# A second batch on scaled 16-bit halves in a two-batch attention and two-layer kernel

## The chip, the cores and the metric

The kernel runs on one core of a Trainium2 chip. The metric is the device time of one execution in microseconds, the median over several runs.

## The reference, cut to what matters

```python
def _attn_ref(q, k, v, proj):                   # q, k, v: (2, 8, 768, 64)
    q_bucket = sum((q @ proj > 0) * powers)     # 6 bits of a sign projection
    k_bucket = sum((k @ proj > 0) * powers)
    scores = where(q_bucket == k_bucket, scale * q @ k.T, -1e9)
    attn = softmax(scores)
    return attn @ v

x = attn_out.transpose(0, 2, 1, 3).reshape(1536, 512)
h = x @ w_in                                    # 512 x 2048
g = where(h >= 1, h, where(h <= -1, 0, (h + 1) ** 2 / 4))
x = g @ w_out                                   # 2048 x 512
h = x @ w_in2
out = (h - tanh(h)) @ w_out2
```

So there are two batches of 768 tokens. Each goes through attention with 8 heads and then through two layers, each of which is a wide product (512 to 2048), a pointwise function and a narrow product (2048 to 512). The four weight matrices arrive in 64 bits and each is cut into 16 blocks of 128 x 512.

## The kernel before, in words

**The work.** Tokens lie along the free dimension, so that a 128 x 768 tile is one chunk of features for one batch, and a matrix product has 128 x 128 weights and 384 moving columns (half of the 768 tokens). The precision of 32 bits is kept by splitting: each operand x becomes a high half and a low half, x = hi + lo, and a product takes three matmuls, hi*hi, hi*lo and lo*hi. For the two layers both halves are of the type `float32r` (the profile writes fp32r, or f32 on the operands of TensorE): weights in `WH`/`WL`, inputs of a layer in `XH`/`XL`, the values between its two products in `GH`/`GL`. ScalarE or VectorE makes the high half by a copy, and VectorE or GpSimd the low half by a subtraction (`copy_hi`, `sub_lo`, `w_split`). Only the product of the attention probabilities with v runs on 16-bit halves (`prep_v16`, `pv`, L631), scaled by a power of two that `prep_v` derives from the largest |v| of a pair of heads.

**The stages.** Attention of the first batch comes first (about 0 to 130 us), then the first batch's two layers with the second batch's attention woven in between, then, from 474 us on, the second batch's two layers alone. In the first batch's layers the units are "i" (a chunk of the wide product, `mats` L866, then `post`) and "o" (a part of the narrow product, accumulated in `accs` by L985). In the second batch the wide product is done in units "s": seven products of half-size blocks take the place of eight (`products`, L897), over sums of input chunks (`TF`, split in `thl`) and sums of weight blocks (`w_mix`, L810, split in `cwhl`), and its results are put together by `plus` (L902). There are 8 "s" units and 16 "o" units per layer.

**Weights.** The first use of a block narrows it from 64 bits (`w_narrow`, L786 to L789) into one of four buffers `WR` and stores the narrowed block in device memory (`scr`); later uses load it from there. A block then is split into `whl(n)`. The first batch has three such slots, and the second batch four, of which it shares three with the first.

**The order.** Every operation is recorded once by `op` or `one`, with the engines that may do it and a planner's cost in ns for each. A packed string, `SCHEDULE`, gives the final order of all items and the engine of each; each engine runs its items in that order. The order was found outside of the kernel by a search, with those costs. All DMAs are issued from SP's queue. `SPINS` puts 64 groups of four small 16-bit matmuls (L1127) at places that the order chooses.

Of the kernel before, what the change touches and what calls it, by code (L numbers as in the profile page):

```python
# [35 lines left out]
    "a})!2z@#ALqgkB`mBl>(d6o*M*uQ1lH%r>)Zn!4r3Y`eh@$_}_Z<QO9Uqs{MButNnbPJ~>u==F8o+@3l>5EiMtI0_qp_oAJjld`y8FEaK^lfnyLc*QonrM~~"
    "?}KaIb8Pi$V%s!toSo(Okh|Bg^!Wa9a>ulU(b3U2#mLY0JUl1_#Xso1@gRF}N1Z*e{p0Kgs9pc8I9a_%$fuu1!S`PaNWZoB3%4Kt#y5`B+g{bLyz&`+X73YJ"
    "8Mhqq-;w-~DfEZV@(0go=IYbVQ_MDLtY6rukB3B2$;9v2?5q5U>vH`mW5ub@Xm(Thg;S@#dF*EKd3J<z{v<oZ7^tskc;H2gJg?;=>eMOqFbKhs$%70jdmhP`"
    "#qlRzApDq_Gc$OYBO*CY4O*Re+(i4+cprA*(U*_u8;*j4=Z-)I;8QHMZ5!JP=`HueJ-6IT4wz!@3SeLRBm3ZX=zxO<AJj4fABG>@&-0S+h7=EOylW&PMxQKf"
    "CL~R;L#7dWxts;Did;W+%f_3N6|l?X{7tqU1Be}KW>v1XVe_6<>SoAH*%Gwc&31+D>_%vtis*EHQ+7po4QvR=_$cu@NKAt2Y_(1x*Ipe#kjrHW+I#gnSX=L*"  # L40
    "P^(b_HJ5kcGD<UK2z~<x3WZ*5kIT2!?(3=XS`BL)DxE;fG}qx!VmYa9TFbKZ`lyl~U^68`ix2hm&=MIO8%r1a6^*k4lydG<B7JICpxohbLNq0-dUMk527yK1"
    "HR9v$e7P)wAWJw_>-DK>wmX*@&oEZ0*eG?cq&@P62~SGesVlbD9r37MTQHpfbCMzNz7q*lDw{QQaUsgtk`SwNg0Dpur7~El#2P!4GTk=s4i|tE+aU%36%bJ>"
    "Bd5Z3x4I9cMAb`7gNzN91>luDTNWf*)0P00a27!*=@f($qumfFpRu7sI7rz|gS&dD=`Khr1VtzIr4VSkP^If=re}2zlrue1S5k~pseALiP-u&fLR(kVxnV=5"
    "vJTdF!$c|AIUej7D{kLW8ihj955w@|klhO|)ZiZIhJT%??LPodDeGg)0Dl__L-!69B&^T(5zc4&R`vBrIbECNhc}qd#<k~WT;Rh~4%y85`uk9i)-?`K4J$Q>"
    "<3eLy?Z=@_ID2?-BV9uW2JU1lKY}y#+9_J!OAbtQ6aJBLj$>?e#oo~oN{8s+ZFs9U?Cn`&s80`0+w~px<mg1T8^NhKlfzDFMDJQQtVgWbVQY3^I}FtO1_A1u"
    "px1P{YSFap4n|6)0wtu4lt*(pPBK9IFqfoo?p2R_qwW;eieXgg?2Iag7*(KX3Z&#Y09hN71Xh`<qQFfD6ls~3Aq44&`zosYA+NfcJKRE<S8YmZrBo`LS80@7"
    "q-n%y;4tc1j^i0R$F!D8qs&PZ8dBvn=Mc50ISW}pJ#YrV$TU1g)v1K`GReQ!Q_2YWG+;W;#c`CxkwMuuqZuVC3>8>5IF@6&kM@<9^%P4(-fp871Tpb#&nGSf"
# [80 lines left out]
def lsh_attention_moe_kernel(ctx: ExitStack, tc: tile.TileContext, qT, kT, vR, projR, eye, w1, w2, w3, w4, out, nbits):  # L128
# [39 lines left out]
    vsm = bufs("vsm", B * NP, [128, 8], F32)  # L168
# [29 lines left out]
    WT = PB[0][:, 3 * 128:4 * 128]  # L198
# [11 lines left out]
    GHX, GLX = GH + Ak, GL + Bk  # L210
# [12 lines left out]
    def late(tag, a, b):  # L223

        if tag not in later:
            later[tag] = sb.tile([128, {"w64": 5120}.get(tag, 2 * KC * SH // 2)], FR, name=f"late_{tag}", tag=tag)
        return later[tag][:, a:b]

    def whl(n):

        return (WH[n], WL[n]) if n < 3 else (late("w64", 3840, 4352), late("w64", 4352, 4864))
# [8 lines left out]
    def halves(t):  # L240
        return t.rearrange("p (a b) -> p a b", a=2)

# [52 lines left out]
    def copy_hi(dst, src, ca, cv, reads, writes, cg=None, by=None):  # L295
        if by is not None:
            op([("A", ca + 95.0, lambda: A.activation(dst, src, AF.Copy, scale=by)),
                ("V", cv + 60.0, lambda: V.tensor_scalar(dst, src, by, None, op0=ALU.mult), 1)], reads, writes)
            return
# [154 lines left out]
    def prep_v16(pr):  # L454
        b, hp, _ = pairs[pr]
        f, fc = v_slot(pr)
        n = b * NP + hp
        s, v = vsm[n], v16[0]
        way = vturn[0] % 2
        vturn[0] += 1  # L460
# [461 lines left out]
    def post(u):  # L922
# [76 lines left out]
        elif len(done) == 2 and b:  # L999
# [5 lines left out]
            else:  # L1005
# [9 lines left out]
                for i in range(3):  # L1015
                    split_t(j, i)
# [160 lines left out]
```

## Time and profile before

| what | value |
|---|---|
| runs | 732.95, 730.7, 732.18 us (median 732.18) |
| span of the profiled execution, first to last instruction | 731.3 us |
| TensorE busy | 716.0 us, 98% |
| TensorE weight loads busy | 666.8 us, 91% |
| VectorE, ScalarE, GpSimd busy | 629.3, 480.6, 343.9 us |

No time of the profiled execution itself is listed apart from its span; the span is 0.9 us under the median of the runs. The end of a matmul is modelled in the trace, so successive matmuls overlap in it; how often they start says more than how long each lasts.

### The profile page before, as it was taken

How to read it: one execution, taken by the hardware profiler on the slowest of the kernel's cores; microseconds unless marked ns; L12 is line 12 of the kernel's file. 1: busy time of each engine (PE TensorE's matmuls, PEld its weight loads, DVE VectorE, ACT ScalarE, POOL GpSimd, SP SyncE). 2: the span in 40 equal slices, each digit the busy share in tenths (PEclk: the TensorE clock that was granted, in tenths of full speed). 3: DMA queues.
4: the chain of work that ended last, by engine and by line, in shares of the span. 5: the costliest groups of instructions: out<-in, count | busy, mean ns of one | idle time of the engine just before them, and what ended most of it. 6: DMA issues, size and time to landing. Idle time of an engine off the chain costs nothing.

```text
span 731.3 us, 12554 instructions
## 1 busy us (share of the span) xinstructions
PE 716.0 (98%) x4512; PEld 666.8 (91%) x4512; DVE 629.3 (86%) x1063; ACT 480.6 (66%) x759; POOL 343.9 (47%) x244
## 2 busy tenths in 40 slices
PE   7899999999999999999999999999999999999998
PEld 6577789777999999999999999999999999999997
DVE  7998998988888999999788887988887898988774
ACT  7998898977978778778776777346544535524311
POOL 5874445565545536453445358541324415253430
PEclk9999999999999999999999999999999999999999
DMA  6997988999999798998888967632211311312112
GB/s 192 233 226 274 246 249 274 210 191 229 261 237 266 185 263 219 227 244 231 223 213 233 246 154 161 169 100 90 72 43 60 100 44 57 88 58 73 44 58 87
DMA packets 165102, 124.91 MB, mean 171 GB/s; under 512 B 127232, under 2 KB 135088, under 8 KB 165040
## 3 DMA queue, kind: packets, MB, share of 16 engines
q1 hardware_dynamic: 165040, 124.12, 65.1%
q8 instruction: 35, 0.57, 0.3%
q14 instruction: 27, 0.22, 0.1%
HBM read 73.47 MB, written 19.95 MB: 128 GB/s over the span
## 4 chain that ended last, share of the span: by engine, by line
PE 86%; DVE 5%; DMA 4%; ACT 3%; issue 1%; POOL 1%; SPq 0%; ACTq 0%; DVEq 0%; POOLq 0%
PE mm L866 52%; PE sbk L897 9%; PE pv L897 5%; PE pv L631 4%; PE ss L506 3%; PE ss L510 3%; PE pb L897 2%; DMA pt<-phl 2%; DVE sm L524 2%; PE pb L1127 1%; PE pv L621 1%; PE mm L593 1%; DMA vr<-in_v 1%; DMA pt<-tmp 1%; ACT p L526 1%
## 5 line engine op out<-in xcount | busy, mean ns | idle before, releaser
L798 POOL TENSOR_TENSOR wl<-wr,wh 128x512 fp32r<-128x512 f32 x69 | 96.0, 1398 | 124.8 <-ACT wh L797 62.2
L866 PE MATMUL mm<-gh,wh 128*128 128x384 f32 x396 | 107.2, 338 | 0.0
L866 PE MATMUL mm<-gh,wl 128*128 128x384 f32 x396 | 105.9, 335 | 0.0
L866 PE MATMUL mm<-gl,wh 128*128 128x384 f32 x396 | 105.8, 335 | 0.0
L526 ACT ACTIVATE p<-ss,sm 128x768 f32<-128x768 f32 x78 | 77.2, 989 | 39.9 <-DVE sm L525 38.4
L532 POOL TENSOR_TENSOR phl<-p,phl 128x768 f16<-128x768 f32 x41 | 70.5, 1720 | 53.6 <-DVE phl L531 20.1
L524 DVE TENSOR_REDUCE sm<-ss 128x1 f32<-128x768 f32 x82 | 78.2, 954 | 14.3 <-PE ss L510 12.2
L797 ACT ACTIVATE wh<-wr 128x512 fp32r<-128x512 f32 x91 | 56.6, 625 | 42.7 <-PE mm L866 23.7
L866 PEld LDWEIGHTS mm<-gh,wh 128*128 128x128 f32 x396 | 71.7, 188 | 1.0 <-issue 0.5
L866 PEld LDWEIGHTS mm<-gl,wh 128*128 128x128 f32 x396 | 72.2, 188 | 0.0
L866 PE MATMUL mm<-xh,wh 128*128 128x384 f32 x256 | 72.0, 341 | 0.0
L866 PEld LDWEIGHTS mm<-gh,wl 128*128 128x128 f32 x396 | 72.0, 188 | 0.0
L866 PE MATMUL mm<-xl,wh 128*128 128x384 f32 x256 | 70.6, 335 | 0.0
L866 PE MATMUL mm<-xh,wl 128*128 128x384 f32 x256 | 70.4, 335 | 0.0
L985 DVE TENSOR_TENSOR accs<-mm,accs 128x768 f32<-128x768 f32 x45 | 42.7, 951 | 9.3 <-PE mm L866 9.0
L306 POOL TENSOR_TENSOR gl<-tmp,gh 128x768 fp32r<-128x768 f32 x20 | 38.8, 1938 | 22.9 <-ACT gh L300 18.7
L789 DVE SCALAR_TENSOR_TENSOR wr<-w,wr 128x512 int32<-128x512 int32 x64 | 44.9, 708 | 4.4 <-ACT wr L787 2.4
L866 PEld LDWEIGHTS mm<-xh,wh 128*128 128x128 f32 x256 | 46.2, 188 | 1.9 <-issue 1.1
L799 DVE TENSOR_TENSOR wl<-wr,wh 128x512 fp32r<-128x512 f32 x59 | 43.8, 744 | 4.4 <-ACT wh L797 4.0
L866 PEld LDWEIGHTS mm<-xl,wh 128*128 128x128 f32 x256 | 46.8, 188 | 0.3 <-DVE xl L307 0.3
L866 PEld LDWEIGHTS mm<-xh,wl 128*128 128x128 f32 x256 | 46.7, 188 | 0.0
L631 PE MATMUL pv<-pt,v 128*64 128x384 f16 x468 | 41.7, 328 | 0.7 <-DMA pt<-tmp 0.7
(340 smaller groups left out, 1844.3 us busy)
## 6 DMA issues: line engine op xcount, KB each, us to landing
w<-in_w SPq DMA_DIRECT2D x64, 512.0 KB, 5.1
qr<-in_qT SPq DMA_DIRECT2D x32, 192.0 KB, 3.2
wr<-scr0i SPq DMA_DIRECT2D x24, 256.0 KB, 2.6
wr<-scr0o SPq DMA_DIRECT2D x24, 256.0 KB, 2.6
krs<-in_kT SPq DMA_DIRECT2D x14, 384.0 KB, 4.2
vr<-in_v SPq DMA_DIRECT2D x12, 384.0 KB, 5.2
scr0i<-wr SPq DMA_DIRECT2D x16, 256.0 KB, 5.0
scr0o<-wr SPq DMA_DIRECT2D x16, 256.0 KB, 3.0
```

The costliest lines, as they stand in the source:

```text
L306: op([("G", cg, lambda: G.tensor_tensor(dst, src, hi.bitcast(F32), op=ALU.subtract)), ("V", cv, lambda: V.tensor_tensor(dst, src, hi.bitca ...
L524: one("V", 870.0, lambda: V.tensor_reduce(z[:, 0:1], s, axis=AX.XY, op=ALU.min), cell, [c])
L526: one("A", 970.0, lambda: A.activation(halves(p), s, AF.Exp, bias=z[:, 2:3], scale=z[:, 3:4], accum_out=LS[lm][:, lk:lk + 1]), cell + [c], ...
L532: lo = [("G", 1600.0, lambda: G.tensor_tensor(hl[:, S:2 * S], p, hl[:, 0:S], op=ALU.subtract)), ("V", 870.0, lambda: V.tensor_tensor(hl[:, ...
L631: T.matmul(ps[j * 64:j * 64 + 64], v[:, kc, a, j, :], PT[n[j]][:, c * KC + kc, :], start=(kc == 0 and i == 0), stop=(kc == KC - 1 and i == 2))
L789: one("V", 600.0, lambda: V.scalar_tensor_tensor(wi, yi, 3, wi, op0=ALU.logical_shift_left, op1=ALU.bitwise_or), [("w64", i, 0)], [("wr", ...
L797: op([("A", 520.0, lambda: A.activation(whl(n)[0], WR[r], AF.Copy)), ("V", 335.0, lambda: V.tensor_copy(whl(n)[0], WR[r]), 1)], [("wr", r) ...
L798: op([("G", 1225.0, lambda: G.tensor_tensor(whl(n)[1], WR[r], whl(n)[0].bitcast(F32), op=ALU.subtract)), ("V", 600.0, lambda: V.tensor_ten ...
L799: ("V", 600.0, lambda: V.tensor_tensor(whl(n)[1], WR[r], whl(n)[0].bitcast(F32), op=ALU.subtract), 1)], [("wr", r), ("wh", n)], [("wl", n)])
L866: T.matmul(ps[:, s + hf, 0:SH], m[:, kc * 128:(kc + 1) * 128], y[:, hf * SH:(hf + 1) * SH], start=(kc == 0 and i == 0), stop=(kc == 3 and ...
L897: T.matmul(sbk(n), m[:, sl], v, start=(j == 0 and i == 0), stop=(j == 1 and i == 2))
L985: one("V", 870.0, lambda: V.tensor_tensor(a, ps, a, op=ALU.add), [pc], c)
```

## The change

The weights, inputs and middle values of the second batch's two layers become float16 halves instead of float32r ones. Since float16 has a narrow range, everything that is split is first scaled by a power of two, and the results are scaled back:

- a largest absolute value is taken of every weight block, once, while it is in `WR` for its last use in the first batch (`w_even`); of all v of the second batch, loaded an extra time in 8 pieces (`later_x`); and of the first layer's result (`vsm[NP + 1]`). `spread` brings each such maximum to all partitions through a small matmul, and `power` makes powers of two of it. `scales_0` and `scales_1` derive the rest in some 40 one-column operations on VectorE;
- each weight block of the second batch is scaled in place before it is split (`w_even`, second part), and the middle values of the second layer are scaled in place as well (`copy_hi(t, t, ..., by=col("ih"))`);
- the other scales ride on operations that were there (`plus`, the accumulation of "o" units, the Relu, the minimum);
- the four `prep_v` of the second batch go, and its v halves use one common scale;
- there are six weight slots of the second batch, none shared with the first batch, two more temporary tiles (`tmp`), and the halves of x, g and w alias the old tiles;
- `SCHEDULE` is a new string. The costs that the planner holds for matmuls of the layers stay 520.5 ns for three.

```diff
+    def spread(src, reads, name, n=1):
+        ps = PB[0][:, 0:128 * n].rearrange("p (a b) -> p a b", a=n)
+        a, b = cols(name + "0", n), cols(name, n)
+        one("V", 100.0, lambda: V.tensor_reduce(a, src, axis=AX.X, op=ALU.max), reads, [("c", name + "0")])
+        def fn():
+            for k in range(n):
+                T.matmul(ps[:, k], a[:, k:k + 1].to_broadcast([128, 128]), unit, start=True, stop=True)
+        one("PE", 150.0, fn, [("c", name + "0"), "unit"], ["pb"])
+        one("V", 230.0, lambda: V.tensor_reduce(b, ps, axis=AX.X, op=ALU.max), ["pb"], [("c", name)])
+    def later_x():
+        f, kh = vx[0], KC // 2
+        for n in range(2 * NP):
+            one("SP", 900.0, lambda n=n: SP.dma_start(out=f, in_=vR[1, n // 2][:, n % 2 * kh:(n % 2 + 1) * kh]), [], ["vx"])
+            one("V", 470.0, lambda n=n: V.tensor_reduce(vsm[NP][:, n:n + 1], f, axis=AX.XYZ, op=ALU.max, apply_absolute_value=True), ["vx"], [("vm", n)])
+        spread(vsm[NP][:, 0:2 * NP], [("vm", n) for n in range(2 * NP)], "v")
+        power("v", 2.0**-11)
...
+    def scales_1():
+        spread(vsm[NP + 1][:, 0:4], [("ym", m) for m in range(4)], "h")
+        times("h", "h", 256.0, "py")
+        times("h", "h", 1.0, ("w1", 0))
+        power("h", 2.0**-13)
+        times("ga1", "ph", 0.25, ("pw1", 1))
...
-        if t < NT and i == 2 and j == 0 and (qh == 0 or b == 0 and by_pe(pr - NP)) and not by_pe(pr):
+        if t < NT and i == 2 and j == 0 and b == 0 and (qh == 0 or by_pe(pr - NP)) and not by_pe(pr):
             prep_v(pr)
...
-        n = w % 3 if w < first_b1 else (w - first_b1 + first_b1 % 3) % 4
+        n = w % 3 if w < first_b1 else 3 + (w - first_b1) % NW16
...
+    def w_even(u):
+        _, l, kind, n = weights[u]
+        if u == last_b0[l, kind, n]:
+            m, f = 2 * l + (kind == "o"), WR[u % len(WR)]
+            one("V", 600.0, lambda: V.tensor_reduce(wst[:, m, n:n + 1], f, axis=AX.X, op=ALU.max, apply_absolute_value=True), ...)
+        if u >= first_b1:
+            f = WR[u % len(WR)]
+            copy_hi(f, f, 520.0, 335.0, [("c", f"iw{l}")], [("wr", u % len(WR))], by=cols(f"iw{l}", 2)[:, (kind == "o"):(kind == "o") + 1])
...
-            one("V", 470.0, lambda: V.tensor_tensor(d, sbk(n), y, op=ALU.add), [SBC[n]] + reads, writes)
+            one("V", 470.0, lambda: V.scalar_tensor_tensor(d, sbk(n), be, y, op0=ALU.mult, op1=ALU.add), [SBC[n], ("c", f"be{l}")] + reads, writes)
...
+                    copy_hi(t, t, 730.0, 470.0, [("c", "ih")], [c], by=col("ih"))
...
+        elif b:
+            one("V", 930.0, lambda: V.scalar_tensor_tensor(a, ps, ga, a, op0=ALU.mult, op1=ALU.add), [pc] + gc, c)
...
+            one("V", 870.0, lambda: V.tensor_reduce(vsm[NP + 1][:, m:m + 1], a, axis=AX.XY, op=ALU.max, apply_absolute_value=True), c, [("ym", m)])
```

## Rows read from the trace of the kernel before

**Rows 1.** The page: span, and busy us (share) x instructions of each engine.
```profile
span 731.3 us, 12554 instructions
PE 716.0 (98%) x4512; PEld 666.8 (91%) x4512; DVE 629.3 (86%) x1063; ACT 480.6 (66%) x759; POOL 343.9 (47%) x244
```

**Rows 2.** Windows: stretch, its length, busy us (instructions) per engine, clock, DMA share, GB/s.
```profile
0.00:200.00 200.00, 189.23 (x1349) 154.45 (x1350) 177.41 (x343) 174.26 (x283) 117.02 (x84) 1.00 0.92 236
...
200.00:474.00 274.00, 273.98 (x1714) 260.94 (x1713) 240.78 (x386) 199.99 (x325) 136.31 (x95) 1.00 0.86 219
...
474.00:605.00 131.00, 129.95 (x749) 129.43 (x748) 112.92 (x185) 62.62 (x89) 42.86 (x33) 1.00 0.23 71
...
605.00:732.00 127.00, 122.84 (x706) 121.96 (x704) 98.19 (x152) 43.78 (x64) 47.72 (x33) 0.99 0.22 67
```

**Rows 3.** Waits of TensorE from 470 us: us in total, times, longest.
```profile
PE mm L866 <- DVE accs L985: 1.1, 1, 1.1
```

**Rows 4.** The chain that ended last: start us, us, what, number of instructions.
```profile
217.29 3.05 PE pv L631 x36
...
474.00 1.04 PE sbk L897 x6
...
585.52 16.95 PE mm L866 x96
...
688.22 9.36 PE mm L866 x54
...
725.75 2.10 PE sbk L854 x12
```

**Rows 5.** Instructions of single lines: ns min/median/max, first and last start us, forms.
```profile
L866 PEld LDWEIGHTS mm<-gh,wh x396: 186/188/192, 107.0 to 724.6; 128*128 128x128 f32 x198
...
L1127 PEld LDWEIGHTS <-warm x256: 95/98/151, 1.1 to 182.4; 128*128 128x128 f16 x128
...
L631 PEld LDWEIGHTS <-v x468: 106/110/110, 39.7 to 471.2; 128*64 128x64 f16 x156
```

**Rows 6.** Windows of L1127 alone: PE and PEld busy us (instructions), clock, DMA.
```profile
3.00:4.00 1.00, 1.00 (x12) 1.00 (x11) 1.00 0.96 344
```

**Rows 7.** VectorE by line and form: xcount | busy us, mean ns | idle before.
```profile
L524 DVE TENSOR_REDUCE sm<-ss 128x1 f32<-128x768 f32 x82 | 78.2, 954 | 14.3 <-PE ss L510 12.2 <-ACT w L786 0.9 <-ACT xh L300 0.2
...
L426 DVE TENSOR_REDUCE vsm<-vr 128x1 f32<-128x768 f32 x8 | 7.6, 948 | 0.7 <-DMA vr<-in_v 0.6
...
L429 DVE TENSOR_REDUCE vsm<-pb 128x1 f32<-128x128 f32 x8 | 2.3, 288 | 0.5 <-PE pb L427 0.3
...
L430 DVE TENSOR_SCALAR vsm<-vsm 128x1 f32<-128x1 f32 x8 | 1.2, 150 | 0.2
```

**Rows 8.** VectorE by line and form, 200 to 474 us only.
```profile
L789 DVE SCALAR_TENSOR_TENSOR wr<-w,wr 128x512 int32<-128x512 int32 x39 | 27.9, 721 | 3.8 <-ACT wr L787 2.4 <-ACT w L786 1.2
L533 DVE TENSOR_TENSOR phl<-p,phl 128x768 f16<-128x768 f32 x23 | 24.3, 1057 | 1.3 <-ACT phl L531 1.1
...
L799 DVE TENSOR_TENSOR wl<-wr,wh 128x512 fp32r<-128x512 f32 x25 | 18.0, 725 | 2.8 <-ACT wh L797 2.6
...
L307 DVE TENSOR_TENSOR gl<-tmp,gh 128x768 fp32r<-128x768 f32 x13 | 13.0, 1010 | 1.1 <-ACT gh L300 1.1
...
L797 DVE CAST wh<-wr 128x512 fp32r<-128x512 f32 x17 | 7.9, 464 | 0.1
```

**Rows 9.** GpSimd by line and form, 200 to 474 us only.
```profile
L798 POOL TENSOR_TENSOR wl<-wr,wh 128x512 fp32r<-128x512 f32 x34 | 46.8, 1380 | 67.6 <-ACT wh L797 40.1 <-DMA w<-in_w 10.9 <-DVE wh L797 10.1
L532 POOL TENSOR_TENSOR phl<-p,phl 128x768 f16<-128x768 f32 x20 | 34.1, 1706 | 25.1 <-issue 9.9 <-ACT phl L531 6.1 <-DVE phl L531 4.1
```

**Rows 10.** ScalarE by line and form, whole span.
```profile
L797 ACT ACTIVATE wh<-wr 128x512 fp32r<-128x512 f32 x91 | 56.6, 625 | 42.7 <-PE mm L866 23.7 <-PE sbk L897 12.2 <-issue 4.7
...
L297 ACT ACTIVATE ab<-qr,cb 128x768 fp32r<-128x768 f32 x31 | 28.7, 927 | 3.6 <-PE ss L510 3.6
```

**Rows 11.** VectorE, accumulation forms with two tensors and with a scalar besides.
```profile
L985 DVE TENSOR_TENSOR accs<-mm,accs 128x768 f32<-128x768 f32 x45 | 42.7, 951 | 9.3 <-PE mm L866 9.0
...
L937 DVE SCALAR_TENSOR_TENSOR tmp<-tmp,p 128x768 f32<-128x768 f32 x8 | 7.6, 951 | 0.0
```

**Rows 12.** DMA issues: KB each, median us from issue to landing.
```profile
vr<-in_v SPq DMA_DIRECT2D x12, 384.0 KB, 5.2
```

More of the change, by code (lines that the diff above doesn't have):

```diff
@@ L60 @@
+    "0zQrVfd"
 )
@@ L225, in late @@
         if tag not in later:
-            later[tag] = sb.tile([128, {"w64": 5120}.get(tag, 2 * KC * SH // 2)], FR, name=f"late_{tag}", tag=tag)
+            later[tag] = sb.tile([128, {"w64": 10240}.get(tag, 2 * KC * SH if tag[:2] == "pt" else 2 * S)], F16, name=f"late_{tag}", tag=tag)
         return later[tag][:, a:b]
     def whl(n):
-        return (WH[n], WL[n]) if n < 3 else (late("w64", 3840, 4352), late("w64", 4352, 4864))
+        if n < 3:
+            return WH[n], WL[n]
+        o = 3840 + 1024 * (n - 3)
+        return late("w64", o, o + 512), late("w64", o + 512, o + 1024)
     def cwhl(z):
@@ L241, in halves, with tmp, x16, g16 @@
         return t.rearrange("p (a b) -> p a b", a=2)
+    def tmp(r):
+        return TMP[r] if r < 2 else late("pt1", 2 * S, 6 * S).bitcast(F32)[:, (r - 2) * S:(r - 1) * S]
+    def x16(x):
+        return late(f"xh{x}", 0, S), late(f"xl{x}", 0, S)
+    def g16(x):
+        a, b = (f"gh{x}", f"gl{x}") if x < NG_ else (f"ak{x - NG_}", f"bk{x - NG_}")
+        return late(a, 0, S), late(b, 0, S)
+    names = {}
+    def col(name):
+        k = names.setdefault(name, len(names))
+        return scal[:, k:k + 1]
+    def full(t):
+        return t if t.dtype == F16 else t.bitcast(F32)
+    def of(t):
+        return t() if callable(t) else t
     pr_raw = TMP[0][:, 0:2 * NB]
@@ L432, in prep_v, with tiny_op, cols @@
         one("V", 70.0, lambda: V.tensor_scalar(s[:, 6:7], s[:, 5:6], EPS, None, op0=ALU.mult), [], [c])
+    MASK, FLOOR = 0x7F800000, 2.0**-80
+    def tiny_op(fn, reads, writes):
+        one("V", 70.0, fn, [("c", r) for r in reads], [("c", w) for w in writes])
+    def cols(name, n=1):
+        if name not in names:
+            names[name] = len(names)
+            names.update({(name, i): 0 for i in range(1, n)})
+        k = names[name]
+        return scal[:, k:k + n]
+    def spread(src, reads, name, n=1):
[6 more added lines that the diff above has]
+        one("PE", 150.0, fn, [("c", name + "0"), "unit"], ["pb"])
+        plan.rows[len(plan.ops) - 1] = 0.3
+        one("V", 230.0, lambda: V.tensor_reduce(b, ps, axis=AX.X, op=ALU.max), ["pb"], [("c", name)])
@@ new lines, in times, with at @@
+    def times(d, x, k, y):
+        def at(v):
+            return cols(v[0], 2)[:, v[1]:v[1] + 1] if isinstance(v, tuple) else cols(v)
+        tiny_op(lambda: V.scalar_tensor_tensor(at(d), at(x), k, at(y), op0=ALU.mult, op1=ALU.mult), [v[0] if isinstance(v, tuple) else v for v in (x, y)], [d])
+    def later_x():
[5 more added lines that the diff above has]
+        power("v", 2.0**-11)
@@ L456, in prep_v16 @@
         f, fc = v_slot(pr)
-        n = b * NP + hp
-        s, v = vsm[n], v16[0]
+        n = ("c", "iv") if b else ("vsm", hp)
+        s, v = col("iv") if b else vsm[hp][:, 5:6], v16[0]
         way = vturn[0] % 2
@@ L1016, in post @@
                     split_t(j, i)
+                if m == 3:
+                    scales_1()
         elif len(done) == 2:
@@ L1085, in pump @@
             elif p in leads:
-                if not reused or p + 1 >= n or before[p] >= first or before[p + 1] >= first:
+                if not reused or p + 1 >= n or before[p] >= first or before[p + 1] >= first or snum[p] > 1 and order_s[snum[p] - 2] >= first:
                     return
```

226 lines of the change are left out of this document (141 added, 85 removed).

## The prediction

> **What bounds the kernel now.** I read the page first, then the windows by stage, the waits of TensorE, the chain of waits, and last the groups of each engine. The page gives TensorE 98% of the span, VectorE 86% [rows 1]. The windows show where it is true: from 0 to 200 us TensorE idles 10.8 us; from 200 to 474 us it idles 0.02 us, although VectorE is busy for 240.8 of 274 us; from 474 us to its last matmul it idles about 1 us [rows 2], the one wait listed there [rows 3]. The reader is to see that after 200 us nothing waits but the end of TensorE's own stream.
>
> The second batch's layers begin at 474 us and end with the last matmul, 727.85 us [rows 4]. By the code a unit "s" has 7 products x 2 x 3 = 42 matmuls and a layer 8 of them, and an "o" unit 4 x 3 x 2 = 24 and a layer 16: 336 + 384 = 720 a layer, 1440 in all. The chain gives their pace: 9.36 us / 54 = 173.3 ns, and 16.95 / 96 = 176.6 with small waits in it [rows 4]. I use 173.4: 1440 x 173.4 = 249.7 us of the 253.9. So TensorE sets this stage alone, at 173.4 ns for 384 columns, which at the granted clock of 1.00 (its level of 2.4 GHz) [rows 2] are 160 ns of columns. Something else holds each matmul for 13 ns more.
>
> **The weight load holds it.** Every one of these matmuls loads its 128 x 128 weights anew, and the load rows show 188 ns for float32r and 98 ns for 16 bits, almost without spread [rows 5]; the loads are busy for 99% of the stage [rows 2]. The pace is the length of a load less 15 ns: 188 - 15 = 173. The 16-bit row gives the same sum: in the groups of L1127, 128 columns each (53 ns of columns), 12 start in each us, 83.3 ns, and 98 - 15 = 83 [rows 5, 6]. I conclude that the float32r stream runs at the pace of loads and that 16 bits would take the load out of the way (83 against 160).
>
> **What the 16-bit matmuls give.** No row shows a 16-bit matmul of 128 weights and 384 columns. From below it is bounded by its columns, 160 ns. From above: the v products (L631) are 16-bit, 384 columns, and run in pairs of 64 weights each side by side, 36 in 3.05 us, 169.4 ns a pair with its two loads [rows 4, 5]. I take 163, nearer to the columns, since a pair has two loads of 110 ns and this stream one of 98. Then 1440 x (173.4 - 163) = 15.0 us; the ends are 19.3 (at 160) and 5.8 (at 169.4).
>
> The Trainium skill, page TensorE: Matmul & The Clock Gate, section Back-to-back issue gap, gives an isolated gap of columns / 2.4 + 2.5 ns. That would be 162.5 ns here and 15.7 us; no row here has that case.
>
> **What is added before 474 us.** VectorE alone can do the maxima of 64 weight blocks. A maximum over 768 columns takes 954 ns and over 128 columns 288 [rows 7], so 1.04 ns a column and 688 ns for 512: 44.0 us. The 8 maxima of v pieces (384 columns): 8 x 0.55 = 4.4. Three `spread` at about 1 us and some 32 one-column operations at 0.15 [rows 7]: 8. Away go four `prep_v`, each 948 + 288 + 3 x 150 ns [rows 7]: 6.8. Net +50 us on VectorE. Nearly all lies in 200 to 474 us, where a block has its last use in the first batch: about +46 on 240.8, which is 287 of 274 us [rows 2]. As it stands that does not fit. What can move by the code: copies to ScalarE, 17 of L797 (7.9 us, at 625 ns there) [rows 8, 10] and others like it, and subtractions to GpSimd, 23 of L533 (24.3 us, at 1706 there), 25 of L799 (18.0 us, at 1380), 13 of L307 [rows 8, 9]. ScalarE has 74 and GpSimd 138 us free in this stretch [rows 2]. Moving 8 us of copies and 25 of subtractions brings VectorE to 254 of 274 and GpSimd to about 184. So it is covered, with less slack for TensorE's buffers than before (93% instead of 88%). I charge 4 us; the ends are 0 and, if only 20 us are moved usefully where a queue wants them, 267 of 274 with waits in every unit: about 14.
>
> Extra loads of v: 8 of 192 KB, half of a v load each, which lands in 5.2 us [rows 12]; 1.6 MB on a stretch that moves some 220 GB/s [rows 2] is 7 us of transfer beside a DMA share of 0.86. They are needed only before the second batch's v halves and scales, and I charge nothing; the cover gone, the eight one behind the other in one buffer are some 8 x 4 us, well inside of 200 us of the first batch's layers. SP has 8 more issues ahead of its transposes; charged under the 4 us.
>
> **What is added from 474 us.** Scaling 64 weight blocks in place: on ScalarE at 625 to 720 ns, 46 us. Scaling 16 middle tiles: on ScalarE 927 each [rows 10], 15 us. ScalarE has 106 of 254 us busy [rows 2] and would have 167. VectorE gets four maxima (3.8 us) and `scales_1` (about 2 us); the accumulations keep their price, for a form with a scalar takes 951 ns as the plain one does [rows 11]. So VectorE has 211 + 6 = 217 us [rows 2] in what was 254 and would be 239: 91%, up from 83%. GpSimd is free for 164 us [rows 2]. TensorE waited for VectorE once before, 1.1 us [rows 3]; I charge 2 us (0 to 6). `scales_1` stands between the first layer's last accumulation and the first split of the second; TensorE has the first three "s" units of 42 matmuls, some 7 us each, to do meanwhile. Six slots instead of four, none of them the first batch's, and two more `tmp` make waits rarer; nothing charged. The matmuls of `spread`, 6 against 4 before, are nothing. After the last matmul stands the same addition and transfer, 3.4 us.
>
> **The sum.** From the profiled span: 731.3 - 15.0 + 4 + 2 = 722.3; the runs' median is 0.9 above the span, and the sum then is 723. A new order moves also the first 200 us, where 10.8 us of idle TensorE can shrink or grow; I put -1 and forecast **722 us**. Under 2.2 us (0.3%) a measurement cannot tell a difference.
>
> **The rivals.**
> *VectorE becomes the bound before 474 us.* For it: 287 us asked of 274, and every block waits in `WR` for its maximum before it is split and the next can be loaded. Against it: 138 us of free GpSimd. It decides when less than about 15 us of work leave VectorE. If the 13 us of excess stand, that is 732 - 15 + 13 = 730, and up to 742 if the waits around each maximum cost as much again. 0.17.
> A rule of the Trainium skill speaks for it (SBUF — State Buffer, section Who interferes with whom): VectorE operations with two SBUF inputs, and GpSimd's reads, exclude one another. By it a subtraction moved would still hold VectorE's partner port, 1380 instead of 725 ns, and the room on GpSimd would be smaller than its idle time. The two engines' busy times here, 241 and 136 in 274 us, do overlap by 103 us at the least; the trace does not tell for which operations.
> *The matmuls get no faster:* the 13 ns above the columns belong to every matmul with a fresh load, not to its type. For it: no row with 16 bits and 384 columns. Against it: 98 against 188 ns of load. Then 732 + 4 + 2 = 738. 0.06.
> *The new order also takes most of the early idle time away* (10.8 us, and 23 us of L1127's fillers show room): 722 - 9 = 713. For it: a search may find it. Against it: more work on the engine that early matmuls wait for. 0.12.
> *VectorE becomes the bound after 474 us*, where it stands at 91%: with the subtractions longer or later, most of the 15 us go, and 4 us are charged before: 728 to 733. 0.07.
> *The columns are not the bound either*, and the pace falls to that of loads, 83 ns: 1440 x 90 = 130 us, 602 us. No row shows a start closer than its columns; 0.01. The same page's section on the issue gap states a sustained 131 ns for 512 columns, below its columns, and would be its source; no run here shows it.
>
> **Chances and range.** The forecast case has 0.57, and by its ends (5.8 to 19.3, 0 to 14, 0 to 6, mostly not together) its own range is 716 to 728. Range over cases: 711 to 734, which leaves out the slower half of the first rival, the second and the last. Faster by over 0.3% (below 730): 0.56 of the forecast's 0.57, the order, the columns and half of the late VectorE case, 0.72. Within 0.3%: the rest of these two and 0.05 of the first rival, 0.10. Slower: 0.12 of the first rival and the second, 0.18.
>
> **What the profile after would show.** Loads of `wh` halves near 98 ns and the stage from first L897 to last L854 in 237 to 243 us instead of 253.9 would show the main term right; a pace of 173 would show it wrong. 64 new maxima of 128 x 512 near 688 ns, more subtractions on GpSimd and copies on ScalarE, and TensorE idle of a few us between 200 and 474 us would show the second. Idle TensorE before `plus` or accumulations after 474 us would show the late VectorE case. The prediction is wrong above all if TensorE's idle time before 474 us grows by more than the 15 us.

## The result and the profile after

The changed kernel takes 726.1 us (median of 4 runs, 725.74 to 727.65) against 732.57 us (730.7 to 733.1) for the kernel before: ratio 0.9918, 95% interval 0.99 to 0.9936. It is faster by some 6 us, inside the range, but 4 us slower than the forecast of 722.

The page of the changed kernel (columns as in [rows 1]):

```profile
span 723.9 us, 12721 instructions
PE 702.5 (97%) x4516; PEld 559.4 (77%) x4516; DVE 652.6 (90%) x1067; ACT 539.9 (75%) x849; POOL 458.9 (63%) x329
```

TensorE stays the busiest engine. Its loads fall from 91 to 77% of the span, and its matmul time by 13.5 us, while the span shrinks by only 7.4. The windows of the changed kernel (columns as in [rows 2]):

```profile
0.00:200.00 200.00, 188.61 (x1346) 155.25 (x1347) 178.59 (x342) 174.92 (x287) 132.32 (x94) 0.99 0.94 238
200.00:474.00 274.00, 271.63 (x1696) 258.15 (x1696) 254.58 (x401) 208.23 (x337) 176.41 (x119) 1.00 0.84 218
474.00:605.00 131.00, 127.82 (x780) 77.60 (x775) 120.87 (x185) 89.58 (x130) 85.91 (x67) 1.00 0.27 85
605.00:730.00 125.00, 114.42 (x701) 68.39 (x700) 98.61 (x143) 67.17 (x97) 64.26 (x51) 0.99 0.20 64
```

Between 200 and 474 us TensorE now idles 2.4 us (0.02 before). After 474 us it idles 3.2 us up to 605 us, and 1.0 us from there to its last matmul, which ends at 720.46 us (115.46 less 114.42): 4.2 us, against about 1 before. The second batch's layers begin at 474.4 us and last 246 us instead of 254. Float32r matmuls of the first batch's last units still run inside this stretch, 30 of them (L1006) where the kernel before has 12 (L866), so that 18 x 0.173 = 3 us of its length are older work. The two lines show these matmuls alone (columns as in [rows 6]), after and before:

```profile
474.43:496.00 21.57, 6.73 (x30) 5.25 (x30) 1.00 0.32 99
```

```profile
478.00:485.00 7.00, 2.40 (x12) 2.11 (x12) 1.00 0.27 75
```

The chain that ended last (start us, us, what, number of instructions), for [rows 4]; the loads of the "o" units (ns min/median/max, first and last start us), for [rows 5]; and TensorE's waits from 470 us on, for [rows 3]:

```profile
692.18 3.90 PE mm L1006 x24
...
704.85 3.90 PE mm L1006 x24
...
718.50 1.96 PE sbk L994 x12
```

```profile
L1006 PEld LDWEIGHTS <-late_w x744: 96/98/98, 500.2 to 718.0; 128*128 128x128 f16 x186
```

```profile
PE pb L485 <- DVE scal L481: 1.6, 1, 1.6
PE pv L1039 <- DVE p L1044: 0.9, 2, 0.6
PE sbk L1039 <- DVE p L1044: 0.7, 2, 0.5
PE sbk L1039 <- DVE pt L1044: 0.4, 1, 0.4
```

3.90 us / 24 is 162.5 ns a matmul, against 173.4: the weight load is out of the way. In its place stand short waits for VectorE: the longest is that of the small matmul of `scales_1` (L485) for the reduction ahead of it (L481), and then `plus` (L1044) is late.

VectorE by line and form (xcount | busy us, mean ns | idle before), for [rows 7, 11]: the maxima of the weight blocks, the accumulation of "o" units, `plus`, and the operations `times` on one column and `power` on two.

```profile
L925 DVE TENSOR_REDUCE wst<-wr 128x1 f32<-128x512 f32 x64 | 43.0, 677 | 0.5 <-DMA wr<-scr0o 0.4
...
L1123 DVE SCALAR_TENSOR_TENSOR accs<-mm,scal,accs 128x768 f32<-128x768 f32 x23 | 23.2, 1012 | 6.4 <-PE mm L1006 6.4
...
L1044 DVE SCALAR_TENSOR_TENSOR p<-sbk,scal,p 128x384 f32<-128x384 f32 x32 | 19.5, 610 | 2.6 <-PE sbk L1039 2.2
...
L504 DVE SCALAR_TENSOR_TENSOR scal<-scal 128x1 f32<-128x1 f32 x11 | 5.1, 462 | 0.0
...
L496 DVE TENSOR_SCALAR scal<-scal 128x2 int32<-128x2 int32 x2 | 2.4, 1205 | 0.0
```

The maxima take what was estimated (677 ns, not 688). An "o" accumulation costs 1012 ns where the plain one took 951 [rows 11]. And where [rows 7] has 150 ns for an operation on one column, these two rows, of operations with two tensors (L504) and on two columns (L496), have a mean of 462 and 1205 ns.

### The profile page after: what moved, and what is told of

Same layout as the page of the kernel before. It is cut to its first block, busy times and chain, and to the rows that moved or that the text cites. A ratio compares the mean times of both kernels' runs of the same rounds, so it can differ in the third digit from the quotient of the medians.

```text
span 723.9 us, 12721 instructions
## 1 busy us (share of the span) xinstructions
PE 702.5 (97%) x4516; PEld 559.4 (77%) x4516; DVE 652.6 (90%) x1067; ACT 539.9 (75%) x849; POOL 458.9 (63%) x329
## 4 chain that ended last, share of the span: by engine, by line
PE 55%; DVE 16%; issue 3%; ACT 2%; DMA 2%; SPq 0%; DVEq 0%; ACTq 0%
PE mm L1006 35%; PE sbk L1039 6%; PE pv L1039 3%; PE pv L748 3%; PE ss L623 2%; PE ss L627 2%; PE pb L1039 1%; DVE sm L641 1%; DVE p L1044 1%; DVE accs L1123 1%; DVE phl L650 1%; DVE late_w L934 1%; DVE wr L915 1%; DVE wst L925 1%; DMA vr<-in_v 1%
## 5 line engine op out<-in xcount | busy, mean ns | idle before, releaser
L1006 PEld LDWEIGHTS <-late_w 128*128 128x128 f16 x744 | 72.8, 98 | 48.1
L1006 PE MATMUL mm<-late_gh,late_w 128*128 128x384 f16 x376 | 84.6, 326 | 0.0
L1039 PEld LDWEIGHTS <-late_w 128*128 128x128 f16 x528 | 51.2, 98 | 38.8 <-issue 6.0
L1006 PE MATMUL mm<-xh,wh 128*128 128x384 f32 x256 | 71.4, 339 | 1.7 <-DVE tmp L1103 1.0
L1006 PE MATMUL mm<-gh,wh 128*128 128x384 f32 x256 | 72.5, 344 | 0.2 <-DVE ls L671 0.2
L1006 PE MATMUL mm<-gh,wl 128*128 128x384 f32 x256 | 70.7, 336 | 0.2 <-DVE wl L934 0.2
L1006 PE MATMUL mm<-xh,wl 128*128 128x384 f32 x256 | 70.5, 336 | 0.0
L1006 PE MATMUL mm<-gl,wh 128*128 128x384 f32 x256 | 70.5, 336 | 0.0
L1006 PE MATMUL mm<-xl,wh 128*128 128x384 f32 x256 | 70.3, 335 | 0.0
L933 POOL TENSOR_TENSOR late_w<-wr,late_w 128x512 f16<-128x512 f32 x36 | 48.3, 1346 | 31.3 <-ACT late_w L932 21.0
L1006 PEld LDWEIGHTS mm<-xh,wh 128*128 128x128 f32 x256 | 46.3, 188 | 4.3 <-issue 1.7
L1006 PEld LDWEIGHTS mm<-gh,wh 128*128 128x128 f32 x256 | 46.2, 188 | 2.9 <-issue 1.3
L648 ACT ACTIVATE phl<-p 128x768 f16<-128x768 f32 x51 | 42.5, 835 | 6.7 <-DMA pt<-phl 6.3
L1006 PEld LDWEIGHTS mm<-gh,wl 128*128 128x128 f32 x256 | 46.7, 188 | 0.5 <-DVE wl L934 0.5
L1006 PEld LDWEIGHTS mm<-gl,wh 128*128 128x128 f32 x256 | 46.7, 188 | 0.4 <-DVE gl L337 0.4
L1006 PEld LDWEIGHTS mm<-xh,wl 128*128 128x128 f32 x256 | 46.7, 188 | 0.0
```

The lines of the kernel that those rows point to most:

```text
L648: hi = [("A", 730.0, lambda: A.activation(hl[:, 0:S], p, AF.Copy)), ("V", 470.0, lambda: V.tensor_copy(hl[:, 0:S], p), 1)]
L933: op([("G", 1225.0, lambda: G.tensor_tensor(whl(n)[1], WR[r], full(whl(n)[0]), op=ALU.subtract)), ("V", 600.0, lambda: V.tensor_tensor(whl ...
L1006: T.matmul(ps[:, s + hf, 0:SH], m[:, kc * 128:(kc + 1) * 128], y[:, hf * SH:(hf + 1) * SH], start=(kc == 0 and i == 0), stop=(kc == 3 and ...
L1039: T.matmul(sbk(n), m[:, sl], v, start=(j == 0 and i == 0), stop=(j == 1 and i == 2))
```

## The experiments

Each time is the median of several runs, taken beside runs of the kernel before on the same chip (732.3 to 733.2 us there), with the ratio to it and its 95% interval. More than one chip was used, so kernels are compared by their ratios. The changed kernel's ratio is 0.9918 (0.99 to 0.9936). By the intervals, a difference of two ratios is uncertain by some 0.002, or 1.6 us.

**What the type alone gives, and what the rest takes back.** The first kernel is the one before, in its old order, with only the types changed. The second is the changed kernel in its new order with all scaling left out: no maxima, no scaling in place, no chains, the factors 1.

```diff
 e1, in the kernel before
-later[tag] = sb.tile([128, ...], FR, name=f"late_{tag}", tag=tag)
+later[tag] = sb.tile([128, ...], F16, name=f"late_{tag}", tag=tag)
...
```

> The kernel before, in its old order and with its old items, with one thing changed: the halves of the second batch's layers are float16, unscaled; the scaling is left out, so that small low halves lose bits. Theory 1 (the pace of 162.5 instead of 173.4 ns pays 15.7 us, and the scaling work that came with it charges 8): about 718, 717 to 720. Rival 2 (the loss comes with the new order and not with the scaling): also 717 to 720 here, but then the new order without scaling stays near 724. Rival 3 (the faster stream cannot be fed by VectorE, ScalarE and GpSimd, whatever the scaling): 722 to 726.

```diff
 e6
-one("V", 600.0, lambda: V.tensor_reduce(wst[:, m, n:n + 1], f, ...), ...)
-copy_hi(f, f, 520.0, 335.0, ..., by=cols(f"iw{l}", 2)[...])
-copy_hi(t, t, 730.0, 470.0, ..., by=col("ih"))
+V.memset(scal, 1.0)
...
```

> The changed kernel with all scaling left out: maxima, extra loads of v, small matmuls, one-column operations, scaling in place; all factors are one. Halves stay float16, order and slots stay those of the changed kernel. Theory 1: 717 to 720, as the old order with 16 bits. Rival 2 (the order charges): 723 to 726.

The first took 718.68 us (0.98; 0.9785 to 0.9815), the second 717.94 us (0.9793; 0.9778 to 0.9808). So 16-bit halves alone give some 14.5 us, what the pace promised (1440 x (173.4 - 162.5) = 15.7) less about 1 us. The new order, with its slots and without the four `prep_v` of the second batch, cannot be told from the old one. The scaling costs some 8 us by the times and 9 by the ratios, and the next runs ask which part of it.

**The parts with large busy times.** Four runs leave out, one at a time, the 64 maxima of weight blocks (VectorE 43 us); the maximum of the first layer's result and what spreads it; the scaling of 64 weight blocks in place (ScalarE and VectorE); and the column as factor in `plus` and in the accumulations, with a constant instead.

```diff
 e2
-lambda: V.tensor_reduce(wst[:, m, n:n + 1], f, axis=AX.X, op=ALU.max, ...)
+lambda: None
 e3
-spread(vsm[NP + 1][:, 0:4], [("ym", m) for m in range(4)], "h")
+V.memset(cols("h"), 2048.0)
 e4
-copy_hi(f, f, 520.0, 335.0, ..., by=cols(f"iw{l}", 2)[...])
 e5
-V.scalar_tensor_tensor(d, sbk(n), be, y, op0=ALU.mult, op1=ALU.add)
+V.scalar_tensor_tensor(d, sbk(n), 2.0**-20, y, op0=ALU.mult, op1=ALU.add)
-V.scalar_tensor_tensor(a, ps, ga, a, op0=ALU.mult, op1=ALU.add)
+V.scalar_tensor_tensor(a, ps, 2.0**-20, a, op0=ALU.mult, op1=ALU.add)
```

> The changed kernel without the 64 maxima of weight blocks on VectorE (43 us busy); a constant bound of 0.25 set once takes their place. Theory 1 (the first 474 us lose 3.7 us to VectorE's load): 3 to 4 us faster than the changed kernel, 722 to 723. Rival 2 (order): within 1 us of it, 725 to 726.5, and TensorE's idle time before 474 us stays near 14 us.

> The changed kernel without the maximum of the first layer's result: four maxima, the small matmul of scales_1 and its two reductions are left out, and a constant bound takes their place; the one-column operations that follow stay. Theory 1 (the small matmul stands in TensorE's queue and waits 1.6 to 2 us for VectorE): 1.6 to 2.9 us faster than the changed kernel, 723 to 724.5. Rival (another wait takes its place, since the one-column operations still hold VectorE): 0 to 0.7 us.

> The changed kernel without the scaling in place of the second batch's 64 weight blocks (50 on ScalarE at 712 ns, 14 on VectorE at 596 ns); the weights stay unscaled, so the values come out too small. All scaling out together was worth 8.2 us, its weight maxima alone 0.5. Theory 1a (scaling in place delays each block's split, and VectorE loses 8 us to it): 1 to 2.5 us faster than the changed kernel, 723.5 to 725. Rival (hidden beside TensorE, six slots ahead): within 0.7, 725.4 to 726.8.

> The changed kernel with the factor in plus and in the accumulation of the second batch's o units a constant of the instruction and not a column read from memory; the constant is 2 to the minus 20, so the values are not the reference's. In the changed kernel these take 610 ns (112 of them) and 1012 ns (23) against 554 and 952 before. Theory 1b (the column costs these operations 57 to 60 ns each, 7.8 us of VectorE, and TensorE waits for plus): they fall back to about 554 and 952 ns, and the kernel is 1 to 3 us faster, 723 to 725. Rival: VectorE has room, 0 to 0.7 us.

They took 725.63 us (0.9899; 0.9883 to 0.9914), 727.12 (0.9912; 0.9893 to 0.9931), 726.26 (0.9916; 0.9901 to 0.993) and 725.09 (0.9896; 0.9881 to 0.9912). No interval lies apart from that of the changed kernel: by the ratios the parts are worth 1.4, 0.4, 0.1 and 1.6 us, none of it clear of the noise. The window from 200 to 474 us of the run without the weights' maxima shows how little:

```profile
200.00:474.00 274.00, 272.18 (x1705) 259.10 (x1704) 230.71 (x344) 208.59 (x338) 176.58 (x119) 1.00 0.86 218
```

VectorE is relieved of 24 us there (230.7 for 254.6) and TensorE gains 0.5 us (272.2 for 271.6). In the run with constants `plus` and the accumulation are back at their price of before (xcount | busy us, mean ns), which gives VectorE 6.8 us back (645.8 us busy for 652.6); its profiled span is 0.8 us shorter (723.1 for 723.9), which is within the noise:

```profile
L1123 DVE SCALAR_TENSOR_TENSOR accs<-mm,accs 128x768 f32<-128x768 f32 x23 | 21.9, 952 | 8.8 <-PE mm L1006 8.7
...
L1044 DVE SCALAR_TENSOR_TENSOR p<-sbk,p 128x384 f32<-128x384 f32 x32 | 17.5, 550 | 3.2 <-PE sbk L1039 2.6
```

**The chains.** Next all chains go: the extra loads of v with their maxima, `spread`'s reductions and small matmuls, and every one-column operation; the factors are 1. Weight maxima, scaling in place and columns as factors stay. The second kernel leaves out the weights' and the first layer's maxima as well.

```diff
 e7
-one("V", 70.0, fn, ...)                 # tiny_op; spread and later_x likewise
+one("V", 70.0, lambda: None, ...)
+V.memset(scal, 1.0)
 e8
-lambda: V.tensor_reduce(wst[:, m, n:n + 1], f, ...)
-lambda: V.tensor_reduce(vsm[NP + 1][:, m:m + 1], a, ...)
+lambda: None
```

> The changed kernel without the chains that work out the factors: no extra loads of v and their maxima, no small matmuls with their reductions, no one-column operations; all factors are set to one once. The 64 weight maxima, the four of the first layer's result, the scaling in place and the columns in the accumulations stay. Theory 1c (the chains are what charges most: TensorE lags by 2.6 us more between 474 and 492 us, where VectorE runs 25 of them, some held up to 1.6 us, and by 1.6 us about 600 us): 3 to 5 us faster than the changed kernel, 721 to 723. Rival (each part alone is hidden by the next): 0 to 1.5 us.

> As the one without the chains, and without the 64 and the 4 maxima too; the scaling in place and the columns in the accumulations stay. Theory 1c: 4 to 6 us faster than the changed kernel, 720 to 722; what is left to 717.9 is the scaling in place and the columns. Rival (the scaling in place and the columns charge most): 724 to 725.5.

718.1 us (0.9806; 0.9793 to 0.9819) and 717.75 us (0.9799; 0.9784 to 0.9814). The chains are 8.2 us by the ratios, all of the scaling's cost that is clear of the noise, and the maxima add nothing measurable to them.

The longest wait in the changed kernel, 1.6 us for the small matmul of `scales_1`, is not where they cost. Without that matmul TensorE waits as long a few products later, for a low half of x. Leaving out the late maximum (e3) accordingly gained nothing that could be measured. The longest of TensorE's waits from 470 us on, in the kernel without chains:

```profile
PE sbk L1042 <- DVE late_xl L337: 1.6, 1, 1.6
```

**Late results, or places taken in queues?** If the chains cost because later work waits for their results, a chain that no later work reads is free. If they cost by their places, it is not. Three more runs leave out one part of the chains each: the loads, the one-column operations, `spread`.

```diff
 e9
-a, b = cols(name + "0", n), cols(name, n)
+a, b = dcols(name + "0", n), dcols(name, n)     # all chains write a second tile
+V.memset(scal, 1.0)
 e10
-lambda n=n: SP.dma_start(out=f, in_=vR[1, n // 2][...])
+lambda: None
+V.memset(vx[0], 1.0)
 e11
-one("V", 70.0, fn, ...)                          # tiny_op alone
+one("V", 70.0, lambda: None, ...)
+V.memset(scal, 1.0)
 e12
-def spread(src, reads, name, n=1):
+def spread(src, reads, name, n=1, on=False):     # on: its three parts run
+V.memset(scal, 1.0)
...
```

> All operations of the chains stay (the extra loads of v and their maxima, the reductions and small matmuls of spread, all one-column operations), but they write columns of a second tile that no work of the second batch reads; the scaling, plus and the accumulations read constant columns (1, and a half for the middle tile's clip). Left out: the measured factors alone. Theory one, the chain is late and what reads a factor waits for it: near the kernel without chains, 718 us. Theory two, the chain's operations cost by the places that they take in the queues of SP, VectorE and TensorE, whoever reads them: near the changed kernel, 725 to 726 us. Half of each: about 722 us.

> Only the 8 extra loads of v are out; their 8 maxima run on a tile set once to 1, so the scale of the second batch's v halves comes from a constant maximum. Four of the loads stand in the first 17 us of SP's queue, among the first loads of k and q. Theory one, these loads delay the first products (the changed kernel falls 1.8 to 3 us behind the one without chains within the first 75 us): 723 to 724 us. Theory two, as the prediction said, they charge nothing, and the 8 us are those of the other parts of the chains: 726 us.

> Only the one-column operations are out (power, times and those of scales_0), the factors being constants as in the kernel without chains; the extra loads of v, all maxima, the reductions and the small matmuls of spread stay. Theory one, the one-column operations, which are held up to 1.3 to 1.6 us while a GpSimd operation runs and which later work reads, are the larger part of the 8 us: 720 to 722 us. Theory two, they cost their 0.15 us each off the path, and loads and small matmuls are the rest: 725 us.

> Only spread is out: its 4 short reductions, 6 small matmuls and 4 reductions from PSUM, with their places in TensorE's and VectorE's queues; the one-column operations run on constant columns instead, so the factors are not the measured ones. The extra loads of v stay. Theory one, the small matmuls stop TensorE's queue until VectorE's reduction is there (waits of 1.6 us and less in the trace) and are worth 2 to 3 us: 723 to 724 us. Theory two, a wait taken away there comes back at the next operation, as with the four maxima that were left out: 725 to 726 us.

| left out | us | ratio | interval | below the changed kernel's ratio |
|---|---|---|---|---|
| readers of the chains (e9) | 725.4 | 0.9904 | 0.9887 to 0.9921 | 0.0014 = 1.0 us |
| 8 loads of v (e10) | 724.14 | 0.9885 | 0.9872 to 0.9898 | 0.0033 = 2.4 us |
| one-column operations (e11) | 722.64 | 0.9866 | 0.9853 to 0.9879 | 0.0052 = 3.8 us |
| `spread` (e12) | 724.81 | 0.9892 | 0.9875 to 0.9909 | 0.0026 = 1.9 us |
| all chains (e7) | 718.1 | 0.9806 | 0.9793 to 0.9819 | 0.0112 = 8.2 us |

The chains cost nearly in full when no later work reads them, so it is their places in the in-order queues, and the waits within the chains, that cost; what the readers' waits cost, 1.0 us, is not clear of the noise. The three parts add up, 2.4 + 3.8 + 1.9 = 8.1 us of 8.2, which is closer than their uncertainties allow one to count on. That of `spread` alone overlaps with nothing gained, and the loads' is only just apart from it. The 8 maxima of v, which go with all chains alone, were not measured by themselves.

Where two of the parts cost can be read from one row: the products of "s" units with high halves of x, first and last start. In turn, the changed kernel, the one without the loads, the one without one-column operations, and the one without any chain (x count: ns min/median/max, first to last start us):

```profile
L1039 PE MATMUL sbk<-late_xh,late_w x96: 322/326/337, 474.4 to 697.7; 128*128 128x384 f16 x96
```

```profile
L1040 PE MATMUL sbk<-late_xh,late_w x96: 322/326/337, 472.1 to 695.4; 128*128 128x384 f16 x96
```

```profile
L1042 PE MATMUL sbk<-late_xh,late_w x96: 322/326/338, 474.1 to 694.4; 128*128 128x384 f16 x96
```

```profile
L1042 PE MATMUL sbk<-late_xh,late_w x96: 322/326/337, 471.3 to 691.4; 128*128 128x384 f16 x96
```

Without the loads the stage starts 2.3 us earlier and lasts as long (223.3 us from first to last): what they cost lies before it. Without one-column operations it starts 0.3 us earlier and lasts 3.0 us less (220.3). Without any chain both appear: 3.1 us earlier, and 3.2 us less (220.1).

**The loads.** The timeline of SP's queue (start us, us, line) in the changed kernel, cut to four of the extra loads and to later marks of the same queue, and then these marks in the kernel without them:

```profile
3.10 0.43 SPq L510 DMA_DIRECT2D vx<-in_v  x1
3.57 0.43 SPq L353 DMA_DIRECT2D krs<-in_kT  x1
...
8.21 0.38 SPq L510 DMA_DIRECT2D vx<-in_v  x1
9.77 0.33 SPq L357 DMA_DIRECT2D krs<-in_kT  x1
...
11.91 0.33 SPq L510 DMA_DIRECT2D vx<-in_v  x1
...
17.01 0.33 SPq L510 DMA_DIRECT2D vx<-in_v  x1
...
25.08 2.76 SPq L357 DMA_DIRECT2D krs<-in_kT  x2
...
35.42 0.43 SPq L897 DMA_DIRECT2D w<-in_w  x1
```

```profile
23.73 2.73 SPq L358 DMA_DIRECT2D krs<-in_kT  x2
...
34.03 0.44 SPq L898 DMA_DIRECT2D w<-in_w  x1
```

The new order puts four of the eight extra loads into the first 17 us, between the first loads of k and q, for which the first products wait. At 25 and at 35 us the queue is 1.4 us later than without them, and the stage of the second batch 2.3 us. The 0.9 us between need not be the loads': in this execution of the changed kernel the granted clock of TensorE fell to 0.50 (its level of 1.2 GHz) from 51.4 to 54.8 us, shortly after a stretch, 48 to 50 us, in which it was busy for 0.26 us, and in the one without the loads it was 1.00 throughout. The windows of the changed kernel (columns as in [rows 2]):

```profile
48.00:50.00 2.00, 0.26 (x2) 0.00 (x0) 1.94 (x6) 2.00 (x4) 1.86 (x3) 1.00 0.91 170
51.40:54.80 3.40, 3.40 (x16) 3.31 (x15) 1.50 (x4) 1.78 (x3) 3.26 (x3) 0.50 1.08 218
```

So 1.4 us of the loads' price are seen where they stand, and the rest is open. Whether the issue slots in SP's queue delay the first products, or the bytes moved beside them, was not separated either.

**The one-column operations.** Leaving out all of them takes VectorE from 652.6 us and 1067 instructions to 645.4 us and 1035, of which 3 are new settings of constants: VectorE's busy time falls by 7.4 us for 35 operations (the settings take 0.2). Their own durations add up to more, 13.1 us, for operations of VectorE overlap a little in the trace, and others run longer or shorter without them. And the time is not evenly spread: 18 of them, with one tensor and one column, take 0.15 us each as in [rows 7], and the other 17, with two tensors or two columns, 0.61 us on average. In the timeline of the changed kernel around one of them (start us, us, engine, line):

```profile
609.09 0.61 DVE L1044 SCALAR_TENSOR_TENSOR p<-sbk,scal,p 128x384 f32<-128x384 f32 x1
609.29 1.64 POOL L953 TENSOR_TENSOR late_pt<-phl,late_pt 128x768 f16<-128x768 f32 x1
...
609.62 1.32 DVE L504 SCALAR_TENSOR_TENSOR scal<-scal 128x1 f32<-128x1 f32 x1
...
610.86 0.60 DVE L1044 SCALAR_TENSOR_TENSOR p<-pv,scal,p 128x384 f32<-128x384 f32 x1
611.39 0.60 DVE L1044 SCALAR_TENSOR_TENSOR p<-sbk,scal,p 128x384 f32<-128x384 f32 x1
...
611.52 0.32 PE L1039 MATMUL pv<-late_xh,late_w 128*128 128x384 f16 x1 [0.58 <-DVE p L1044]
```

The operation, on one column of two tensors, starts while GpSimd subtracts, and ends with it, at 610.94 and 610.93 us: 1.32 us instead of 0.15. `plus` behind it in VectorE's queue comes 1.2 us late, and TensorE, which needs the PSUM that `plus` empties, waits 0.58 us. Meanwhile the `plus` operations of 0.61 us, which read PSUM, run beside GpSimd unhurt: one of them overlaps the first 0.4 us of this subtraction.

This place is the smaller part. The loads of the "o" units in the kernel without these operations, beside the same row of the changed kernel above (500.2 to 718.0), show a lead of 2.4 us at 500 us and 3.3 at the end:

```profile
L1009 PEld LDWEIGHTS <-late_w x744: 96/98/98, 497.8 to 714.7; 128*128 128x128 f16 x186
```

So the lead of 0.3 us at 474 us grows by 2.1 up to 500 us, where nine of the 35 operations run (and not 25, as the expectation of e7 has it). How much of that is due to the holding, and how much to their plain 0.15 us each ahead of `plus`, was not separated.

The Trainium skill, page SBUF — State Buffer, section Who interferes with whom, says that VectorE and GpSimd share a second port pair, held by one of them at a time. This row agrees with it. Not every operation on one column is held, though; the last section has the rows.

## Why the prediction was right, and where it was off

**The main term was right, and sized almost exactly.** The conclusion that float32r matmuls run at the pace of their loads held: with loads of 98 ns the pace is 162.5 ns where 163 was taken, 15.7 us against 15.0, and 14.5 us in the run with nothing but the types changed. The stage itself lasted 246 us, and not the 237 to 243 that the prediction gave as the sign: it holds 3 us more of the first batch's matmuls, and 3 us more of idle time.

The Trainium skill's page TensorE: Matmul & The Clock Gate, section Back-to-back issue gap, gave the same 162.5 ns by its formula, and the trace agrees with it. Its sustained 131 ns for 512 columns, the source of the last rival, was not seen: the chain rows show no pace below 162.5 ns for 384 columns.

**The loads of engines were right.** VectorE was to have 254 of 274 us between 200 and 474 us, and has 254.6; GpSimd about 184, and has 176; VectorE about 217 us after 474, and has 219. The rival with VectorE as the bound before 474 us fell: TensorE idles 2.4 us there, and without the maxima 1.8.

**The step that failed** is the pricing of the scale chains. The prediction said of the extra loads of v "I charge nothing", of the matmuls of `spread` that they "are nothing", priced the one-column operations at 0.15 us of VectorE's time, and hid `scales_1` behind TensorE's next three units. Leaving out the chains gives 8.2 us back: 2.4 for the loads, 3.8 for the one-column operations and, less surely, 1.9 for `spread`.

For the loads, the price was taken on an average ("well inside of 200 us of the first batch's layers"), but the order put half of them where the first products wait for data and TensorE has its idle time. For the one-column operations, the row of 150 ns in [rows 7] is of another form, one tensor and one column. That form is not held: 13 of the 24 such operations of `prep_v` in the kernel before run within a GpSimd operation, in 139 to 155 ns. 17 of the 35 new ones have two tensors or two columns, and their mean is 0.61 us. The prediction had a rule for VectorE's operations with two tensors beside GpSimd, in its first rival, and used it for moved subtractions only. The argument that the results are in time held as far as the run with unread chains shows, but was beside the point, since `plus` stands behind them in VectorE's queue.

**The charge of 4 us before 474 us** was put on the maxima, and was wrong in its cause: without them nothing measurable is gained, while the loads put TensorE back by 1.4 us within the first 25 us, and the stage from 474 us by 2.3. The total charged (4 + 2 - 1 = 5 us) was short of the 8 us found, 3.2 us of the 4.1 by which the forecast missed. Another 0.5 is that the run for the types gave 14.5 and not 15, and 0.4 that the kernel before has a median of 732.57 us beside it and not 732.18. That these terms close the sum is luck, since a difference of two runs is uncertain by more than 1 us; and it is luck too that charges made for other causes stood in for most of the chains' price.

**Right in substance:** the 2 us after 474 us. TensorE's idle time there grew by 3.2 us, in part through `plus`, as the late VectorE case has it, but the run without one-column operations shows these as the cause, not the busy share. **Wrong without effect:** "the accumulations keep their price". A column as factor costs 57 to 60 ns more than none (610 for 550, 1012 for 952), 6.8 us of VectorE's time, and 0 to 2 us in the end. The row taken for it, L937 in [rows 11], had no operand in PSUM and no column. **The order** gave nothing that could be told from none; its -1 was within that.

Kernels with every factor 1 are the fastest of the study, 718 us against 726 and 732 (e1, e6, e7, e8). They take the operands unscaled, and float16 then holds only what lies in its narrow range, so they are other kernels rather than a better order of this one. A version that keeps the scaling, with the loads of v moved behind the first products and the factors computed where GpSimd rests, needs a new order of all items and was not tried; as an estimate from the runs above it could win back 2 to 6 us.

## What to carry to other kernels

When a stream of matmuls starts as often as its weight loads end, a type with a shorter load pays until the columns bound it, and one row of the load's duration and one of the pace say how much. In a kernel of in-order queues that is nearly full, price a new operation by its place and not by its length: 43 us of maxima in VectorE's slack cost nothing measurable, while 35 small operations, 13 us in all, and eight loads cost 6 us. And take the price of such an operation from a row of the same form (how many tensors, how many columns) next to a busy GpSimd.

## What the runs showed of the hardware that was not expected

A small operation of VectorE on one or two columns takes some 140 to 160 ns alone, and up to 1.57 us when a GpSimd subtraction runs beside it. Whether it is held goes by its form in these traces. In the changed kernel 11 operations with two tensors (L504) or with two columns (L496 and others) began within a GpSimd operation, and all 11 ended with it, 16 to 28 ns later. Ten with one tensor and one column began so as well, and took 136 to 214 ns. The rows of two such lines (ns min/median/max, first and last start us):

```profile
L504 DVE SCALAR_TENSOR_TENSOR scal<-scal x11: 147/160/1323, 469.7 to 631.7; 128x1 f32<-128x1 f32 x11
```

```profile
L496 DVE TENSOR_SCALAR scal<-scal x5: 136/141/1569, 188.9 to 614.4; 128x1 int32<-128x1 int32 x3, 128x2 int32<-128x2 int32 x2
```

One that is not held and one that is, both of a single tensor, the first on one column and the second on two (the timeline):

```profile
493.06 1.64 POOL L953 TENSOR_TENSOR late_w<-phl,late_w 128x768 f16<-128x768 f32 x1
...
493.74 0.14 DVE L497 TENSOR_SCALAR scal<-scal 128x1 int32<-128x1 int32 x1
...
553.79 1.65 POOL L336 TENSOR_TENSOR late_gl<-tmp,late_gh 128x768 f16<-128x768 f32 x1
553.89 1.57 DVE L496 TENSOR_SCALAR scal<-scal 128x2 int32<-128x2 int32 x1
```

A subtraction on VectorE over two GpSimd operations (the timeline):

```profile
312.18 1.28 POOL L933 TENSOR_TENSOR wl<-wr,wh 128x512 fp32r<-128x512 f32 x1
313.43 1.66 POOL L649 TENSOR_TENSOR phl<-p,phl 128x768 f16<-128x768 f32 x1
```

```profile
312.32 3.58 DVE L650 TENSOR_TENSOR phl<-p,phl 128x768 f16<-128x768 f32 x1
```

This subtraction takes 0.95 us by the median of its 18; started inside a GpSimd operation, it gave way to that one and to the next, 1.28 + 1.66 us, and ended 0.8 us after them.
